# Attention with beacons and a gated feed-forward: start of the weight loads, the gate of the second batch's loads, and the cuts of the third batch

## Chip, cores and metric

The kernel runs on one core of one Trainium2 chip. The metric is the device time of one execution in microseconds; the times shown are medians of several runs. Besides, one execution was profiled, and every duration of a single instruction is from that one.

## The reference

Eight batches of eight heads, 576 positions, head size 64, and 16 beacon keys and values ahead of each sequence. The scores are causal over the 576 positions and open over the beacons. The result of all heads is put side by side and goes through a gated feed-forward with 1536 hidden columns.

```python
k_all = np.concatenate([beacon_k, k], axis=2)
v_all = np.concatenate([beacon_v, v], axis=2)
scores = scale * np.matmul(q, k_all.transpose(0, 1, 3, 2))
scores = np.where(causal, -1e9, scores)
a = np.exp(scores - scores.max(-1, keepdims=True))
a /= a.sum(-1, keepdims=True) + 1e-09
x = np.matmul(a, v_all)          # then [B*S, H*D] = [4608, 512]
out = (np.maximum(x @ w_gate, 0.0) * (x @ w_val)) @ w_out
```

## The kernel before

**Order of the work.** The whole kernel is a list of tasks, each with the engines that may run it, a cost in us, the tasks it depends on, the buffers it holds and a priority. When the program is built, a planner (class `Plan`, lines 134 to 244) plays the tasks through with these costs: it always takes the task that can start first, at equal times the one with the lowest priority number, and puts it at the end of its engine's queue. On the chip each engine works through its queue strictly in that order. So the costs in the code decide the order, and the chip decides the times: a task whose input comes later than planned holds up all that stands behind it on its engine. Where PE has a planned gap before 100 us, the planner puts in filler matmuls (line 874), which compute nothing.

**Loads.** All loads of q, k and v, the transposing DMAs and the stores are issued by SP, in one queue. For each batch there are four pairs of heads for k and four for q (`load_pair`, 256 KB in packets of 1 KB, so 256 packets), one rest each for k and q (`load_rest`, 80 rows of 8 heads in 256 B packets, so 640, in two DMAs each) and five for v (`load_v`, up to 128 rows of 8 heads, 1024 packets; the first one in two DMAs, beacon and v). Their order is "KQ0011v2233vvvv" for batch 1 and on: K and Q are the rests, a digit is a pair (first k, then q), v the next of the five. They land in seven shared fp32 stage buffers. From there POOL (for batch 0 POOL or DVE) rounds them to bf16: line 455 for k and q, line 415 (`copy`) for v. PE transposes k and q (line 467), ACT or DVE evict them (lines 411 and 413) into `kT` and the block-diagonal `diag`.

**Weights.** The nine weight blocks (three each of gate, value and output, in the order g0, v0, g1, v1, g2, v2, o0, o1, o2) are fetched and cast to bf16 by DMAs that POOL issues (line 428). The planner may issue block i no earlier than W_FROM + W_STEP * i. The rests of batch 1 wait for a weight: in the plan both rests have the weight `GATE` as dependency, and in the program the first DMA of the k rest has a semaphore wait on it (lines 524 to 526). `GATE` is ("v", 1), the fourth weight.

**Attention.** For each batch and each head pair the positions are cut into steps A to E of 128 rows (two heads of 64), and a step F for the last positions of all heads. A step is: scores on PE (line 628 or 620), minimum with mask on DVE (line 643), exponential on ACT (line 654), reciprocal (666) on DVE and normalisation on POOL, for batch 0 on POOL or DVE (673). The probabilities are then transposed, for batch 0 by PE (708), for the others by one transposing DMA per group of steps (719), and multiplied by v (729), and the result is copied to `xT` (411 or 413). `STEPS` says which steps form a group: for batches 0 and 1 "AB", then "C", then "D", "E", each for all four pairs. A batch that is not in `STEPS` does all five steps of a pair in one group, no earlier than 39 us per batch in the plan.

**Feed-forward.** For each batch the first 512 positions are cut by `CUTS` into parts of columns; a part can begin once the attention of those columns is in `xT` for all pairs. For each of 12 hidden blocks PE runs four matmuls with the gate weight and four with the value weight (line 796), ACT the relu (800), DVE the product (804). The projection (816) works on 128 rows at a time. The last 64 positions of four batches together form one more part. Its priority stands behind all attention, so it fills PE.

Of the kernel before, what the change touches and what calls it, by code (L numbers as in the profile page):

```python
# [20 lines left out]
RANK1 = -8.1  # L21
AHEAD = 2.0
W_ISSUE = 0.8
W_MOVE = 3.2
W_FROM = 14.0
W_STEP = 3.3
SHARED = 1.5
FILLED = 100.0
FILL = 0.8
FILL_FROM = 2.9  # L30
# [8 lines left out]
NORM_B = 1  # L39
N_DVE = 0.3  # L40
F_MOST = 3
GATE = "v", 1
SC_MOST = 4
SC_FIRST = 6
V_MOST = 3
# [3 lines left out]
N_ST = 7  # L49
N_OSB = 4  # L50
STEPS = {0: [(["AB"], 0.0, 0.6), (["C"], 2.4, 0.6), (["D", "E"], 4.8, 0.6)],
         1: [(["AB"], 0.0, 0.6), (["C"], 2.4, 0.6), (["D", "E"], 4.8, 0.6)]}
CUTS = {0: (240,), 1: (368,)}
LAST_PARTS = 2
FIRST_MOST = 3
PACE0 = 0.0
# [77 lines left out]
class Plan:  # L134
# [7 lines left out]
    def add(self, engines, cost, run, deps=(), holds=(), prio=0.0, lag=None, part=False, lazy=0.0, after=0.0, move=0.0):  # L142
        t = Task(engines if isinstance(engines, tuple) else (engines,), cost, run, deps, holds, prio, lag, part, lazy, move)
        t.ready = after
        for d in t.deps:
            d.users.append(t)
        self.tasks.append(t)
        return t

    def order(self):  # L150
# [10 lines left out]
        wire = cast = 0.0  # L161
# [16 lines left out]
        while True:  # L178
            best = None
            for e in queue:  # L180
                for t in queue[e]:
# [3 lines left out]
                    at, could = times  # L185
# [20 lines left out]
            t.start, t.engine = at, e  # L206
            cost = t.cost
            if e == "DMA":
                issue, move = cost
                rest = max(0.0, cast - max(wire, at + 0.3))  # L210
                cast += min(move, rest / SHARED)
                move += min(rest, SHARED * move)
                if issue > 1.2:
                    wire = max(wire, at + 0.3) + move
                    free[e] = max(at + issue, wire - 0.2)
                else:
                    free[e] = at + issue
                    wire = max(wire, at + issue) + move
                end = max(wire, free[e]) + 1.9
            elif t.move:  # L220
                free[e] = at + cost
                cast = max(cast, free[e] + 0.7) + t.move
                end = cast + 2.0
            else:
                if isinstance(cost, dict):
                    cost = cost[e]
                if e == "PE":
                    cost += SWITCH * (t.part != part)
                    part = t.part
                free[e] = end = at + cost  # L230
            for h in t.holds:
                h.users -= 1
                if h.users == 0:
                    h.slots.give(end + (0.1 if e == "DMA" else LAGS[e] if t.lag is None else t.lag), h.tile)
            done.append(t)
            for u in t.users:
                u.ready = max(u.ready, end + (LAGS[e] if t.lag is None else t.lag))
# [10 lines left out]
def kernel(  # L248
# [184 lines left out]
    def heads(src, b, s0, sl):  # L433
        return src[b, :, s0:s0 + sl, :].rearrange("h s d -> s h d")
# [6 lines left out]
    def new_batch(b, prio, work):  # L441
# [18 lines left out]
        def turned(h16, rows, ca, prio, users):  # L460
# [8 lines left out]

            return ps, add("PE", c_pe(4 * rows), turn, (ca, on_ident), (h16, ps), prio[1])  # L470

        eng = ("POOL", "DVE") if b == 0 else ("POOL",)
        cost = {"POOL": 0.6, "DVE": 0.55}
        MAIN = 4 * P
# [2 lines left out]
        def load_pair(kind, p, prio):  # L477
# [2 lines left out]
            st = Hold(stage_s, 2)  # L480

            def fetch(_):
                nc.sync.dma_start(st.tile.rearrange("p (h e) -> p h e", h=2),
                                  src[b, 2 * p:2 * p + 2, s0:s0 + MAIN, :].rearrange("h (p j) d -> p h (j d)", j=4))

            ld = add("DMA", (0.5, 0.87), fetch, (), (st,), prio[0])
            dst = t.kT if kind == "k" else t.diag
            h16, ca = rounded(dst, st, P, neg_scale if kind == "q" else 1.0, prio, ld,
                              lambda t_: t_.rearrange("p (j h d) -> p h j d", h=2, j=4))
# [23 lines left out]
        def load_rest(kind, prio):  # L513
# [5 lines left out]
            def fetch(_):  # L519
                s3 = st.tile.rearrange("p (h d) -> p h d", h=H)  # L520
                at = 0
                for src, s0, n in pieces:
                    one = nc.sync.dma_start(s3[at:at + n], heads(src, b, s0, n))  # L523
# [26 lines left out]
        def load_v(c, prio):  # L550
            st = Hold(stage_s, 2)
            rows = min(P, SK - P * c)

            def fetch(_):
                s3 = st.tile.rearrange("p (h d) -> p h d", h=H)
                if c == 0:
                    nc.sync.dma_start(s3[:Nb], heads(beacon_v, b, 0, Nb))
                    nc.sync.dma_start(s3[Nb:], heads(v, b, 0, P - Nb))
                else:
                    nc.sync.dma_start(s3[:rows], heads(v, b, P * c - Nb, rows))  # L560
# [347 lines left out]
```

## Time and profile before

| what | us |
|---|---|
| runs: median of 3 (lowest, highest) | 424.46 (424.33, 424.82) |
| the profiled execution | 423.93 |
| its span, first to last instruction | 422.2 |

In a row of the table by stage stand the stretch and its length in us, then for each engine its busy time with the number of instructions, then the granted clock of PE as a share of full speed, the mean share of the DMA engines and GB/s. In a row of the time line stand the start and the length in us, engine, line, operation, output and inputs, the shape and the number of instructions merged; in brackets, how long the engine had been idle and who released it. A row of the DMA view gives the KB of one transfer and the time from its issue to its landing.

### The profile page before, as it was taken

To read this page: it belongs to the slowest core of one execution; us is meant where nothing else is said; L and a number is where in the kernel's file an instruction comes from. 1 tells how busy PE (TensorE), PEld (TensorE's weight loads), DVE (VectorE), ACT (ScalarE), POOL (GpSimd) and SP (SyncE) were. 2 spreads that over 40 slices of the span, in tenths; PEclk is the share of its full clock that TensorE was granted. 3 is DMA by queue.
4 is the path that set the end of the run, shared out by engine and by line. 5 is a ranking of instruction groups with operands and counts; after the bars stand their busy time and mean duration, and the time that the engine had idled before them with its cause. 6 is when DMAs were issued, how large, how long until landed. Compare 5 with 4: busy or idle time off the path is not lost.

```text
span 422.2 us, 10131 instructions
## 1 busy us (share of the span) xinstructions
PE 399.7 (95%) x3194; PEld 234.9 (56%) x3229; DVE 318.5 (75%) x1147; ACT 290.0 (69%) x957; POOL 226.5 (54%) x421
## 2 busy tenths in 40 slices
PE   7878799999999999989999999999999999999994
PEld 4655677646657445544555765455454544444483
DVE  6788798888999987888988989889897334243251
ACT  5677799877988889778978998886788133023030
POOL 6676467766876868486866786686755000000000
PEclk9999999999999999999999999999999999999999
DMA  7999926999999999989997899898954600110112
GB/s 210 217 241 234 201 59 118 215 205 219 135 274 215 180 175 240 206 159 231 243 193 190 206 242 184 162 244 217 221 94 79 152 27 2 50 50 2 50 51 50
DMA packets 172486, 68.00 MB, mean 161 GB/s; under 512 B 146704, under 2 KB 167952, under 8 KB 172432
## 3 DMA queue, kind: packets, MB, share of 16 engines
q1 hardware_dynamic: 167680, 62.64, 70.0%
q0 software_dynamic: 4752, 4.72, 6.7%
q8 instruction: 25, 0.41, 0.4%
q14 instruction: 29, 0.24, 0.2%
HBM read 38.54 MB, written 9.44 MB: 114 GB/s over the span
## 4 chain that ended last, share of the span: by engine, by line
PE 51%; POOL 2%; DVE 1%; DMA 1%; issue 1%; SPq 1%; ACT 0%; POOLq 0%; DVEq 0%
PE f L796 27%; PE f L816 15%; PE f L729 3%; PE f L628 3%; PE f L467 2%; POOL pb L673 1%; DMA st<-in_q_dram 1%; PE f L620 1%; PE f L758 1%; SPq L523 0%; DVE osb L413 0%; DVE f L643 0%; POOL h L455 0%; SPq L560 0%; PE f L623 0%
## 5 line engine op out<-in xcount | busy, mean ns | idle before, releaser
L673 POOL TENSOR_SCALAR pb<-pb,small 128x448 bf16<-128x448 bf16 (+8 forms) x237 | 125.8, 545 | 58.1 <-DVE small L666 42.1
L654 ACT ACTIVATE pb<-f,small 128x512 bf16<-128x512 f32 (+3 forms) x272 | 137.5, 519 | 19.8 <-DVE small L643 11.6
L643 DVE CUSTOM_DVE_ANT_0 f<-f,mask 128x64 f32<-128x64 f32 (+7 forms) x256 | 112.4, 476 | 7.8 <-PE f L628 6.4
L800 ACT ACTIVATE g<-f 128x512 f32<-128x512 f32 (+5 forms) x144 | 69.5, 496 | 68.5 <-PE f L796 64.3
L796 PE MATMUL f<-xT,wg_r 128*128 128x512 bf16 (+5 forms) x567 | 109.3, 325 | 1.9 <-DVE xT L413 0.7
L796 PE MATMUL f<-xT,wv_r 128*128 128x512 bf16 (+5 forms) x565 | 110.4, 325 | 0.7 <-ACT pb L654 0.2
L804 DVE TENSOR_TENSOR hT<-g,f 128x512 bf16<-128x512 f32 (+5 forms) x144 | 79.0, 552 | 40.8 <-PE f L796 35.9
L816 PE MATMUL f<-wo_r,hT 128*128 128x512 bf16 (+1 forms) x429 | 100.7, 373 | 0.9 <-issue 0.3
L796 PEld LDWEIGHTS <-wg_r 128*128 128x128 bf16 x576 | 53.6, 98 | 37.8 <-issue 1.4
L796 PEld LDWEIGHTS <-wv_r 128*128 128x128 bf16 x576 | 52.8, 98 | 37.2 <-issue 0.8
L816 PEld LDWEIGHTS <-hT 128*128 128x128 bf16 x444 | 42.0, 98 | 41.7
L455 POOL TENSOR_SCALAR h<-st 128x512 bf16<-128x512 f32 (+1 forms) x80 | 48.9, 616 | 21.8 <-DMA st<-in_q_dram 6.3
L654 ACT ACTIVATION_READ_ACCUMULATOR pb<-f,small 128x1 f32 x272 | 57.9, 213 | 0.0
L628 PE MATMUL f<-kT,diag 128*128 128x64 bf16 (+7 forms) x256 | 47.1, 286 | 0.5 <-DVE kT L413 0.3
L413 DVE COPY osb<-f 128x512 f32<-128x512 f32 (+1 forms) x31 | 21.0, 681 | 27.8 <-PE f L816 22.7
L643 DVE DVE_READ_ACCUMULATOR2_ANT small<- 128x1 f32 x296 | 41.1, 139 | 0.3 <-issue 0.2
L467 PE MATMUL f<-ident,h 128*128 128x128 bf16 (+1 forms) x320 | 29.6, 220 | 6.9 <-POOL h L455 5.8
L467 PEld LDWEIGHTS <-h 128*128 128x128 bf16 (+1 forms) x320 | 21.3, 99 | 20.7 <-POOL h L455 12.8
L729 PEld LDWEIGHTS <-v 128*64 128x64 bf16 (+1 forms) x560 | 21.8, 109 | 14.8 <-issue 8.7
L413 DVE CAST diag<-f 64x512 bf16<-64x512 f32 (+2 forms) x48 | 25.8, 550 | 4.5 <-ACT diag L411 3.2
L640 DVE TENSOR_REDUCE small<-f 128x1 f32<-128x512 f32 x40 | 27.3, 682 | 1.0 <-PE f L620 0.5
L628 PEld LDWEIGHTS <-diag 128*128 128x128 bf16 x256 | 20.2, 98 | 13.9 <-DVE diag L413 0.6
(64 smaller groups left out, 357.3 us busy)
## 6 DMA issues: line engine op xcount, KB each, us to landing
st<-in_k_dram SPq DMA_DIRECT2D x32, 256.0 KB, 4.2
st<-in_q_dram SPq DMA_DIRECT2D x32, 256.0 KB, 4.1
out_dram<-osb SPq DMA_DIRECT2D x32, 256.0 KB, 2.4
st<-in_v_dram SPq DMA_DIRECT2D x24, 256.0 KB, 4.8
st<-in_v_dram SPq DMA_DIRECT2D x8, 224.0 KB, 5.3
wg_r<-in_moe_w_gate_dram POOLq DMA_DIRECT2D x3, 512.0 KB, 9.7
wv_r<-in_moe_w_val_dram POOLq DMA_DIRECT2D x3, 512.0 KB, 9.5
wo_r<-in_moe_w_out_dram POOLq DMA_DIRECT2D x3, 512.0 KB, 9.6
```

The lines of the kernel that those rows point to most:

```text
L413: nc.vector.tensor_copy(dst, src)
L455: e.tensor_scalar(order(h16.tile)[:rows], st.tile[:rows] if rows < P else st.tile.rearrange("p (h j d) -> p h j d", h=2, j=4), by, 1.0, AL ...
L467: nc.tensor.matmul(to, h16.tile[:rows, a * P:(a + 1) * P], ident[:rows, :rows], start=True, stop=True)
L628: nc.tensor.matmul(view(i), t.diag.tile[:, p, j * P:j * P + P], kT[:, p, :n], start=True, stop=True)
L643: nc.vector.tensor_tensor_reduce(out=view(i), in0=view(i), in1=msk, scale=1.0, scalar=small["t"][:, 0:1] if name in "EF" else 3.0e38, op0= ...
L654: nc.scalar.activation(ph.tile.rearrange("p a n -> p (a n)")[:, a:a + n], view(i), AF.Exp, bias=small["t"][:, low:low + 1], scale=-1.0, ac ...
L673: (nc.gpsimd if x.engine == "POOL" else nc.vector).tensor_scalar(one, one, small["t"][:, 8 + i:9 + i], 1.0, ALU.mult, ALU.mult)
L729: nc.tensor.matmul(ps.tile[64 * hh:64 * hh + 64, d0:d0 + w], t.v.tile[:rows, c, D * h:D * h + D], rhs(64 * hh), start=(c == 0), stop=(c == ...
L796: nc.tensor.matmul(to, w_r[:, ki, nf * P:(nf + 1) * P], x, start=(ki == 0), stop=(ki == KM - 1))
L800: r = add("ACT", c_act(w), lambda _, psg=psg, g=g: nc.scalar.activation(g.tile[:, :w], psg.tile[:, :w], AF.Relu), (a,), (psg, g), -1000 + ...
L804: hid.append(add("DVE", c_dve(w), lambda _, psv=psv, g=g, nf=nf: nc.vector.tensor_mul(hT[nf].tile[:, c0:c0 + w], g.tile[:, :w], psv.tile[: ...
L816: nc.tensor.matmul(ps.tile[:, :w], hT[nf].tile[:, t0:t0 + P], wo_r[:, nf, n0:n0 + w], start=(nf == 0), stop=(nf == NF - 1))
```

## The change

Weights: W_FROM goes from 14.0 to 17.0 and the planned move of one weight from 3.2 to 3.1 us. Gate: `GATE` becomes ("v", 0), the second weight, and now all 15 loads of batch 1 depend on it in the plan, not the two rests alone; in the program the DMAs of the pairs, the rests and the first or only DMA of each v load have the semaphore wait. Loads beside weights: the planner lengthened a load by up to 1.5 times its own move while a weight was still to move; now it lengthens it by 0.006 us for each of its packets, in proportion to how much of the load falls beside weights. Batches: the first part of batch 1's feed-forward ends at column 240 instead of 368, batch 2's feed-forward is cut at 240 too, and batch 2's attention is done in two groups per pair, "AB" for all pairs and then "C", "D", "E", with no earliest start. The stored end time `t.end` is not used.

```diff
-W_MOVE = 3.2
-W_FROM = 14.0
+W_MOVE = 3.1
+W_FROM = 17.0
 W_STEP = 3.3
-SHARED = 1.5
+PACKET = 0.006
...
-GATE = "v", 1
+GATE = "v", 0
...
 STEPS = {0: [(["AB"], 0.0, 0.6), (["C"], 2.4, 0.6), (["D", "E"], 4.8, 0.6)],
-         1: [(["AB"], 0.0, 0.6), (["C"], 2.4, 0.6), (["D", "E"], 4.8, 0.6)]}
-CUTS = {0: (240,), 1: (368,)}
+         1: [(["AB"], 0.0, 0.6), (["C"], 2.4, 0.6), (["D", "E"], 4.8, 0.6)],
+         2: [(["AB"], 0.0, 0.6), (["C", "D", "E"], 2.4, 0.6)]}
+CUTS = {0: (240,), 1: (240,), 2: (240,)}
...
             if e == "DMA":
-                issue, move = cost
-                rest = max(0.0, cast - max(wire, at + 0.3))
-                cast += min(move, rest / SHARED)
-                move += min(rest, SHARED * move)
+                issue, move, *packets = cost
+                slow = PACKET * (packets[0] if packets else 128)
+                both = min(1.0, max(0.0, cast - max(wire, at + 0.3)) / (move + slow))
+                cast += move * both
+                move += slow * both
...
+        gate = (weight_in[GATE],) if b else ()
+
+        def gated(one):
+            if b == 1:
+                tc.add_manual_dep(one.ins, weight_dma[GATE].ins.name, mybir.DependencyInfo(
+                    mybir.DependencyClass.Sync, mybir.DependencyReason.DATA), reason="weights first")
...
-            ld = add("DMA", (0.5, 0.87), fetch, (), (st,), prio[0])
+            ld = add("DMA", (0.5, 0.87, 256), fetch, gate, (st,), prio[0])
...
-                    one = nc.sync.dma_start(s3[at:at + n], heads(src, b, s0, n))
-                    if b == 1 and kind == "k" and at == 0:
-                        tc.add_manual_dep(one.ins, weight_dma[GATE].ins.name, mybir.DependencyInfo(
-                            mybir.DependencyClass.Sync, mybir.DependencyReason.DATA), reason="weights first")
+                    gated(nc.sync.dma_start(s3[at:at + n], heads(src, b, s0, n)))
                     at += n
 
-            ld = add("DMA", (1.3, 0.96), fetch, (weight_in[GATE],) if b == 1 else (), (st,), prio[0])
+            ld = add("DMA", (1.3, 0.96, 640), fetch, gate, (st,), prio[0])
...
-            ld = add("DMA", (1.1 if c == 0 else 0.55, 1.54 * rows / P), fetch, (), (st,), prio[0])
+            ld = add("DMA", (1.1 if c == 0 else 0.55, 1.54 * rows / P, 8 * rows), fetch, gate, (st,), prio[0])
```

In the plan the loads of the later batches depend on that weight as well (`if b`); in the program only batch 1's have the wait.

More of the change, by code (lines that the diff above doesn't have):

```diff
@@ L234, in order @@
                     h.slots.give(end + (0.1 if e == "DMA" else LAGS[e] if t.lag is None else t.lag), h.tile)
+            t.end = end
             done.append(t)
@@ L482, in fetch @@
             def fetch(_):
-                nc.sync.dma_start(st.tile.rearrange("p (h e) -> p h e", h=2),
-                                  src[b, 2 * p:2 * p + 2, s0:s0 + MAIN, :].rearrange("h (p j) d -> p h (j d)", j=4))
-            ld = add("DMA", (0.5, 0.87), fetch, (), (st,), prio[0])
+                gated(nc.sync.dma_start(st.tile.rearrange("p (h e) -> p h e", h=2),
+                                        src[b, 2 * p:2 * p + 2, s0:s0 + MAIN, :].rearrange("h (p j) d -> p h (j d)", j=4)))
+            ld = add("DMA", (0.5, 0.87, 256), fetch, gate, (st,), prio[0])
             dst = t.kT if kind == "k" else t.diag
@@ L556, in fetch @@
                 if c == 0:
-                    nc.sync.dma_start(s3[:Nb], heads(beacon_v, b, 0, Nb))
+                    gated(nc.sync.dma_start(s3[:Nb], heads(beacon_v, b, 0, Nb)))
                     nc.sync.dma_start(s3[Nb:], heads(v, b, 0, P - Nb))
                 else:
-                    nc.sync.dma_start(s3[:rows], heads(v, b, P * c - Nb, rows))
-            ld = add("DMA", (1.1 if c == 0 else 0.55, 1.54 * rows / P), fetch, (), (st,), prio[0])
+                    gated(nc.sync.dma_start(s3[:rows], heads(v, b, P * c - Nb, rows)))
+            ld = add("DMA", (1.1 if c == 0 else 0.55, 1.54 * rows / P, 8 * rows), fetch, gate, (st,), prio[0])
             t.rows["v", c] = add(eng, cost, lambda x: copy(x.engine, t.v.tile[:rows, c, :], st.tile[:rows]),
```

## The prediction

> **What bounds the kernel now.** I read the page first, then the busy time of the engines by stage, then who waited for whom on PE, POOL and DVE in the first 65 us, and last each load's issue and landing there.
>
> ```profile
> span 422.2 us, 10131 instructions
> PE 399.7 (95%) x3194; PEld 234.9 (56%) x3229; DVE 318.5 (75%) x1147; ACT 290.0 (69%) x957; POOL 226.5 (54%) x421
> ```
>
> PE is busy for 95% of the span, so a gain must come from PE time in which it does nothing or does filler work. The table by stage says where that is. I cut the span at 33.6 us (first feed-forward matmul), 64.8 us (first feed-forward matmul on the second part of batch 0) and 340 us (attention is over). The first four rows are all instructions; the last is the filler matmuls of line 874 alone, which compute nothing.
>
> ```profile
> 0.00:33.60 33.60, 26.83 (x263) 18.27 (x264) 26.07 (x122) 23.27 (x68) 21.23 (x45) 1.00 1.03 224
> 33.60:64.80 31.20, 26.37 (x305) 20.05 (x305) 25.33 (x97) 26.04 (x92) 20.12 (x34) 1.00 0.85 153
> 64.80:340.00 275.20, 269.92 (x2211) 155.96 (x2236) 238.13 (x883) 222.05 (x764) 185.15 (x343) 1.00 0.93 192
> 340.00:422.20 82.20, 76.55 (x421) 40.62 (x426) 28.94 (x48) 18.59 (x36) 0.00 (x0) 1.00 0.11 36
> ...
> 0.00:33.60 33.60, 17.08 (x100) 9.80 (x100) 1.00 1.03 224
> ```
>
> After 64.8 us PE idles 275.20 - 269.92 = 5.3 us up to 340 us and 5.7 us behind it, most of that the last output. There PE is the bound: work that arrives earlier only lengthens its backlog. Before 64.8 us PE idles 6.8 + 4.8 = 11.6 us, and up to 33.6 us it runs 100 fillers: there the attention of batch 0 feeds PE, and a stall of that chain moves the end. The clock (the 1.00 behind POOL) is full throughout, so no term is a clock term.
>
> Three idle stretches of PE are large, and each has a late load behind it. The next rows are of the time line, by engine: PE, then DVE, then POOL, then SP's issues.
>
> ```profile
> 23.71 0.36 PE L729 MATMUL f<-xT,v 128*64 128x128 bf16 x6 [1.45 <-DVE xT L413]
> 33.60 0.98 PE L796 MATMUL f<-xT,wg_r 128*128 128x240 bf16 x8
> 37.23 0.34 PE L708 MATMUL f<-ident,xT 128*128 128x128 bf16 x3 [1.72 <-POOL xT L673]
> 51.34 0.32 PE L467 MATMUL f<-ident,h 80*128 80x80 bf16 x4 [2.14 <-POOL h L455]
> 56.68 0.44 PE L628 MATMUL f<-kT,diag 128*128 128x64 bf16 x4
> 64.80 1.09 PE L796 MATMUL f<-xT,wg_r 128*128 128x272 bf16 x8
> ...
> 22.16 0.42 DVE L413 CAST v<-st 80x512 bf16<-80x512 f32 x1 [1.70 <-DMA st<-in_v_dram]
> ...
> 34.47 0.73 POOL L415 TENSOR_SCALAR v<-st 128x512 bf16<-128x512 f32 x1 [3.19 <-DMA st<-in_v_dram]
> 50.66 0.61 POOL L455 TENSOR_SCALAR h<-st 80x512 bf16<-80x512 f32 x1 [3.66 <-DVE small L643]
> ...
> 13.87 1.36 SPq L560 DMA_DIRECT2D st<-in_v_dram  x1
> 15.32 0.61 SPq L483 DMA_DIRECT2D st<-in_k_dram  x1
> 19.73 0.42 SPq L558 DMA_DIRECT2D st<-in_v_dram  x1
> 36.11 0.61 SPq L523 DMA_DIRECT2D st<-in_k_dram  x1
> ```
>
> The landings of those three loads, from the DMA view cut to the moment of their issue, with a load before any weight for comparison (last row):
>
> ```profile
> st<-in_v_dram SPq DMA_DIRECT2D x1, 160.0 KB, 8.3
> ...
> st<-in_v_dram SPq DMA_DIRECT2D x1, 224.0 KB, 14.6
> ...
> st<-in_k_dram SPq DMA_DIRECT2D x1, 128.0 KB, 13.6
> ...
> st<-in_v_dram SPq DMA_DIRECT2D x1, 256.0 KB, 6.9
> ```
>
> Stall A: batch 0's last v load, issued at 13.87, lands 8.3 us later at 22.2, where DVE had waited 1.70 us with the scores queued behind that copy; PE idles 1.45. Stall B: batch 1's first v load, issued at 19.73, lands 14.6 us later at 34.3; POOL stood 3.19 us before its copy at 34.47, batch 0's normalisations queued behind it, and PE idles 1.72. Stall C: batch 1's k rest, issued at 36.11, lands at 49.7, its beacon piece just after; POOL stood 3.66 us before the rounding at 50.66. The view names a DVE instruction as releaser there, but the landing fits and I put it down to the load. PE idles 2.14. In sum **5.31 us of PE idle** comes from loads that ran beside weights.
>
> **The change, part by part.** *Weights and gate.* These rows are the second weight's issue, which is the new gate, and the fourth's, the old gate; then SP's wait for the old gate and the second weight's landing.
>
> ```profile
> 17.62 0.79 POOL L428 DMA_DIRECT2D wv_r<-in_moe_w_val_dram  x1
> 25.77 0.79 POOL L428 DMA_DIRECT2D wv_r<-in_moe_w_val_dram  x1
> ...
> SPq L523 <- DMA wv_r<-in_moe_w_val_dram: 5.4, 1, 5.4
> ...
> wv_r<-in_moe_w_val_dram POOLq DMA_DIRECT2D x1, 512.0 KB, 9.5
> ```
>
> With W_FROM at 17.0 and a step of 3.3 the first weight goes out at about 17.0 and the second at 20.3. Batch 0's last v load then has neither a weight nor batch 1's loads beside it and should land in at most the 6.9 us of its larger neighbour: 20.8 instead of 22.2, 1.4 us earlier, which is nearly all of stall A. I take -1.45 (bounds -1.7, DVE's wait, and 0).
>
> The second weight lands at 20.3 + 9.5 = 29.8 at the latest and, with the engines nearly to itself, I expect 27 to 28. Until then SP issues nothing: behind its waiting instruction stand all 15 loads of batch 1, and behind those batch 2's and the transposes, the first at 63.3. So batch 1's first load goes out some 12 us later than 15.32, but its k and q rest, first in the list, some 8 us earlier than 36.11. Stall B goes: the first v load now stands behind rests and four pair loads. Stall C goes, since the rest is due by 28 + 13.6 = 41.6, 9 us before 50.66. -1.72 and -2.14.
>
> What is late next? POOL rounds batch 1's pairs in order among batch 0's normalisations, and those loads now run later and still beside seven weights. The planner's new rule (0.006 us for each packet beside a weight) expects 7.7 us for a v load of 1024 packets where the old one expected at most 3.9, 4.8 against 2.4 for a rest, 2.4 against 2.2 for a pair. The copies that came too early in POOL's order are just those of the loads whose expectation grows, so the order errs less, but not by nothing. Bounds: 0, and 5.31 again; I take one stall like B, **+1.72**, the row that is also a copy put ahead of its load.
>
> Three rows for what follows: batch 1's first values on PE, two of its evictions on ACT, and the busy times from 40 to 50 us.
>
> ```profile
> 68.89 0.36 PE L729 MATMUL f<-xT,v 128*64 128x128 bf16 x6
> 28.60 1.19 ACT L411 CAST diag<-f 64x512 bf16<-64x512 f32 x2
> 40.00:50.00 10.00, 9.03 (x98) 7.09 (x96) 9.84 (x37) 9.92 (x33) 4.34 (x7) 1.00 1.22 199
> ```
>
> Cover for lateness itself: batch 1's first scores ran at 56.68 and its first values at 68.89; when 64.8 comes PE has 96 x 0.116 + 36 x 0.216 = 18.9 us of batch 0's second part (strides below) in front of it. A shift by 12 us is covered by that; it costs where it blocks POOL's queue, not as missing work.
>
> Batch 1's evictions on ACT and DVE, those of 28.60 among them, move behind 33 us. ACT gets them back where it is as full (9.92 of 10 us), so I count 0; bounds -2.4 us (the two of that row and two more like them, ahead of batch 0's last exponentials) and +2.4.
>
> *Cuts.* The first row below is a run of eight matmuls, as are the rows at 33.60 and 64.80 above; the groups by shape give the mean ns of one, with its fill and drain. The stride is the run less one matmul's own time, over 7.
>
> ```profile
> 155.82 1.89 PE L796 MATMUL f<-xT,wg_r 128*128 128x512 bf16 x8
> ...
> L796 PE MATMUL f<-xT,wg_r 128*128 128x512 bf16 x279 | 70.0, 379 | 1.2 <-DVE xT L413 0.7
> L796 PE MATMUL f<-xT,wg_r 128*128 128x272 bf16 x48 | 6.9, 279 | 0.0
> L796 PE MATMUL f<-xT,wg_r 128*128 128x240 bf16 x48 | 6.4, 265 | 0.2 <-ACT pb L654 0.2
> ...
> L804 DVE TENSOR_TENSOR hT<-g,f 128x512 bf16<-128x512 f32 x72 | 49.3, 686 | 32.4 <-PE f L796 28.9 <-ACT pb L654 1.4 <-ACT g L800 0.8
> L804 DVE TENSOR_TENSOR hT<-g,f 128x272 bf16<-128x272 f32 x12 | 5.2, 436 | 1.0 <-PE f L796 0.8
> L804 DVE TENSOR_TENSOR hT<-g,f 128x240 bf16<-128x240 f32 x12 | 4.7, 401 | 2.1 <-PE f L796 1.5 <-PE f L874 0.4 <-ACT xT L411 0.2
> ```
>
> 512 columns: (1.89 - 0.379) / 7 = 216 ns. 240: (0.98 - 0.265) / 7 = 102; 272: (1.09 - 0.279) / 7 = 116. Batch 2 replaces 96 strides of 216 by 96 of 102 + 116 = 218: +0.2 us on PE. Batch 1 had 368 + 144 columns and gets 240 + 272; the stride goes with the columns (0.42 to 0.43 ns each in all three), so I count nothing. DVE gains 12 x (401 + 436 - 686) = 1.8 us, and ACT, with as many more relus, by my estimate about as much; from 64.8 to 340 us they idle 37 and 53 us. If that cover were gone, it would show as up to some 2 us.
>
> *Third batch in two steps.* Per head pair one transposing DMA of 25 blocks becomes one of 6 and one of 21.
>
> ```profile
> L719 SPq DMA_TRANSPOSE pTb<-pb x28: 1603/4018/6822, 81.2 to 327.7; - x28
> L719 SPq DMA_TRANSPOSE xT<-xT x8: 1209/1220/1919, 63.3 to 85.2; - x8
> ```
>
> SP gains four issues of 1.22 us (the six-block median), less what 21 blocks save on 25: between 2 and 5 us on a queue that mostly waits for POOL. The same score, softmax and value instructions run; batch 2's attention also loses its planned earliest start (78 us and later) and can fill holes before batch 1's is done. PE is bound there, so I count 0; bounds -1 (batch 2's first half no longer waits for the whole attention, part of the 5.3 us idle) and +2 (its work put in front of batch 1's on a full DVE).
>
> **Sum.** -1.45 - 1.72 - 2.14 + 1.72 + 0.2 = -3.4 us. The profiled execution took 423.93 us (span 422.2, 1.7 around it), 0.5 us under the median of 424.46; I apply the sum to both: 420.5 for a run like the profiled one, **421.0 us** for the median.
>
> **Rivals.** *Slower: the gate starves POOL.* If POOL's order has the first rounding of batch 1 well ahead of its landing, all normalisations of batch 0 stand behind one wait. Stalls B and C cost PE 1.72 / 3.19 = 0.54 and 2.14 / 3.66 = 0.58 us for each us that POOL stood. A POOL wait as long as the delay of the first load (about 12.7 us) would cost 0.58 x 12.7 = 7.4 us, and a second one like B 1.7: 9.1 + 0.2 - 5.3 = +4.0, 428.5 us. It decides from about 5.3 / 0.56 = 9.5 us of new POOL waits on. For it: between the end of batch 0's loads and the gate the engines carry little but two weights, and the same packets then have to move beside the other seven. Against it: stall A goes anyway, and the planner knows of the gate. The Trainium skill, DMA: Bandwidth & Descriptors, section Rules for kernel authors, tells authors to issue a DMA early and to wait late, which speaks against holding 15 loads back; stalls B and C were loads issued early that came late all the same, so this trace does not bear the rule out here, and the rival keeps a chance of its own.
>
> *No difference: the stalls only move.* New waits of about 5 us stand in the place of B and C, for instance for v loads that still land 14 us after issue: -5.3 + 5.1 + 0.2 = 0, 424.5 us. For it: seven of nine weights still overlap batch 1.
>
> *Faster still: batch 0 profits too.* No new stall, and the 2.4 us of ACT evictions leave the way of batch 0's first part: -5.3 - 2.4 + 0.2 = -7.5, 417.0 us. Against it: ACT and DVE are both full from 40 to 50 us and get that work back before 64.8.
>
> **Chances.** Forecast (418.5 to 423.5 by itself) 0.58; slower rival 0.22; no difference 0.10; faster still 0.10. A measurement of this kernel tells about 0.2%, 0.85 us, from no change: faster 0.68, same 0.10, slower 0.22. The range for 8 in 10 runs from 417.0, the sum without new stalls, to 427.0, most of the way to the slower rival.
>
> **What would show it.** Right: on SP no issue between 15.3 and about 27; POOL's first weight near 17; no DVE wait for v near 20; the rounding of 80 rows (L455) for batch 1 before 42; the first 272-column matmul of L796 at about 61 instead of 64.8; PE idle before that down from 11.6 to about 8 us. The idle from there to 340 us should stay near 5.3. Wrong: a POOL wait over 5 us for a load of batch 1 between 28 and 60 us, or a first 272-column matmul no earlier than 64.8. I would also be wrong if the stalls go, but PE idles over 2 us more between 100 and 200 us, where batch 2 changed.

## The result and the profile after

The changed kernel takes **420.64 us** (median of 5, 419.32 to 421.9) against 424.46 (median of 5, 423.68 to 427.24) of the kernel before, run beside it: ratio 0.9895 [0.9854, 0.9936]. Run again, beside the kernel before, it took 421.13 against 425.33, ratio 0.9911 [0.9881, 0.9942] (12 runs). The profiled execution took 420.64 us, span 418.9.

The head of its page, then its table by stage over the cuts that the prediction used (busy time and count of PE, PEld, DVE, ACT, POOL, then the granted clock, DMA share and GB/s):

```profile
span 418.9 us, 10398 instructions
...
PE 402.9 (96%) x3319; PEld 248.4 (59%) x3319; DVE 321.5 (77%) x1174; ACT 289.6 (69%) x953; POOL 226.4 (54%) x422
```

```profile
0.00:33.60 33.60, 29.36 (x266) 20.80 (x266) 27.86 (x130) 24.60 (x75) 20.79 (x45) 1.00 0.93 182
33.60:64.80 31.20, 27.11 (x318) 21.00 (x319) 26.54 (x105) 24.18 (x81) 20.25 (x35) 1.00 1.02 211
64.80:340.00 275.20, 273.04 (x2318) 167.20 (x2317) 239.60 (x896) 223.15 (x766) 185.38 (x343) 1.00 0.93 192
```

PE is idle for 4.2 + 4.1 = 8.3 us up to 64.8 us (before: 11.6) and 2.2 us from there to 340 (before: 5.3). Part of that second difference is bookkeeping: the page of before lists 35 matmuls fewer than weight loads (3194 against 3229), the page of after none, and a missing record reads as idle time.

Now the time line of after, by engine as in the prediction: PE, POOL, DVE, then SP's issues. L803 is the feed-forward matmul, L470 the transposes, L458 the rounding, L418 and L416 the copies, L431 the weights.

```profile
28.70 0.57 PE L803 MATMUL f<-xT,wg_r 128*128 128x240 bf16 x4
34.89 0.32 PE L470 MATMUL f<-ident,h 80*128 80x80 bf16 x4 [1.75 <-POOL h L458]
38.80 0.32 PE L470 MATMUL f<-ident,h 80*128 80x80 bf16 x4 [1.43 <-POOL h L458]
60.88 0.63 PE L803 MATMUL f<-xT,wg_r 128*128 128x272 bf16 x4
...
18.41 0.93 POOL L431 DMA_DIRECT2D wg_r<-in_moe_w_gate_dram  x1
21.34 0.79 POOL L431 DMA_DIRECT2D wv_r<-in_moe_w_val_dram  x1
34.22 0.61 POOL L458 TENSOR_SCALAR h<-st 80x512 bf16<-80x512 f32 x1 [2.56 <-DMA st<-in_beacon_k_dram]
38.14 0.61 POOL L458 TENSOR_SCALAR h<-st 80x512 bf16<-80x512 f32 x1 [2.06 <-DMA st<-in_q_dram]
50.15 0.64 POOL L418 TENSOR_SCALAR v<-st 128x512 bf16<-128x512 f32 x1
...
21.31 0.41 DVE L416 CAST v<-st 80x512 bf16<-80x512 f32 x1
...
8.66 6.94 SPq L567 DMA_DIRECT2D st<-in_v_dram  x4
27.38 0.61 SPq L533 DMA_DIRECT2D st<-in_k_dram  x1
```

Stalls A and B are gone: the last v copy of batch 0 and the first v copy of batch 1 carry no bracket, so nothing was waited for, and SP issues nothing between batch 0's last v load and 27.38. Stall C is gone at its old time, but the rounding that it held, of batch 1's k rest, now stands at 34.22 instead of 50.66 and waits again: POOL stands 2.56 us for the k rest and 2.06 for the q rest, PE 1.75 and 1.43 behind it. The landings (the DMA view, cut to each issue) show both sides: batch 0's last v load took 8.3 us before, the second weight 9.5 and the rest 13.6.

```profile
st<-in_v_dram SPq DMA_DIRECT2D x1, 160.0 KB, 4.9
...
wv_r<-in_moe_w_val_dram POOLq DMA_DIRECT2D x1, 512.0 KB, 6.0
...
st<-in_k_dram SPq DMA_DIRECT2D x1, 128.0 KB, 5.3
```

The first 272-column matmul comes at 60.88 instead of 64.80, 3.9 us earlier; from there to the end it is 358.0 us against 357.4. So the gain was made before 61 us and kept after it. That it was *kept* turned out to be the part that needed explaining.

### The profile page after: what moved, and what is told of

Same layout as the page of the kernel before. It is cut to its first block, busy times and chain, and to the rows that moved or that the text cites. A ratio compares the mean times of both kernels' runs of the same rounds, so it can differ in the third digit from the quotient of the medians.

```text
span 418.9 us, 10398 instructions
## 1 busy us (share of the span) xinstructions
PE 402.9 (96%) x3319; PEld 248.4 (59%) x3319; DVE 321.5 (77%) x1174; ACT 289.6 (69%) x953; POOL 226.4 (54%) x422
## 4 chain that ended last, share of the span: by engine, by line
PE 77%; DVE 7%; ACT 5%; DMA 5%; POOL 3%; issue 2%; SPq 1%; POOLq 0%; DVEq 0%; ACTq 0%
PE f L803 38%; PE f L823 21%; PE f L635 6%; PE f L736 5%; PE f L470 3%; DMA st<-in_q_dram 2%; DVE diag L416 2%; DVE f L650 2%; PE f L627 1%; ACT xT L661 1%; POOL pb L680 1%; DMA xT<-xT 1%; PE f L881 1%; DVE hT L811 1%; ACT pb L661 1%
## 5 line engine op out<-in xcount | busy, mean ns | idle before, releaser
L680 POOL TENSOR_SCALAR pb<-pb,small 128x512 bf16<-128x512 bf16 (+8 forms) x220 | 119.3, 556 | 71.1 <-DVE small L673 52.6
L661 ACT ACTIVATE pb<-f,small 128x64 bf16<-128x64 f32 (+4 forms) x256 | 130.9, 524 | 19.8 <-DVE small L650 12.8
L807 ACT ACTIVATE g<-f 128x512 f32<-128x512 f32 (+3 forms) x156 | 71.6, 470 | 71.2 <-PE f L803 69.2
L650 DVE CUSTOM_DVE_ANT_0 f<-f,mask 128x256 f32<-128x256 f32 (+7 forms) x256 | 112.6, 475 | 8.0 <-PE f L635 6.2
L803 PE MATMUL f<-xT,wv_r 128*128 128x512 bf16 (+3 forms) x624 | 113.0, 314 | 0.2 <-ACT xT L661 0.2
L803 PE MATMUL f<-xT,wg_r 128*128 128x512 bf16 (+3 forms) x624 | 110.5, 314 | 0.1
L811 DVE TENSOR_TENSOR hT<-g,f 128x512 bf16<-128x512 f32 (+3 forms) x156 | 80.2, 519 | 33.9 <-PE f L803 30.1
L803 PEld LDWEIGHTS <-wg_r 128*128 128x128 bf16 x624 | 59.7, 98 | 32.7 <-issue 0.2
L803 PEld LDWEIGHTS <-wv_r 128*128 128x128 bf16 x624 | 58.2, 98 | 34.4 <-issue 1.8
L458 POOL TENSOR_SCALAR h<-st 128x512 bf16<-128x512 f32 (+1 forms) x80 | 48.9, 617 | 15.0 <-DMA st<-in_q_dram 5.7
L635 PE MATMUL f<-kT,diag 128*128 128x256 bf16 (+7 forms) x256 | 48.4, 291 | 1.7 <-DVE diag L416 1.4
L650 DVE DVE_READ_ACCUMULATOR2_ANT small<- 128x1 f32 x296 | 41.2, 139 | 0.2
L416 DVE COPY osb<-f 128x512 f32<-128x512 f32 (+1 forms) x30 | 20.3, 679 | 24.0 <-PE f L823 23.4
L470 PE MATMUL f<-ident,h 128*128 128x128 bf16 (+1 forms) x320 | 30.1, 222 | 4.8 <-POOL h L458 4.4
L416 DVE CAST diag<-f 64x512 bf16<-64x512 f32 (+2 forms) x54 | 26.3, 505 | 7.9 <-PE f L470 4.4
L470 PEld LDWEIGHTS <-h 128*128 128x128 bf16 (+1 forms) x320 | 22.5, 101 | 16.1 <-POOL h L458 7.8
L661 ACT ACTIVATE xT<-f,small 128x64 bf16<-128x64 f32 (+3 forms) x64 | 27.4, 444 | 2.8 <-DVE small L650 2.2
```

What stands on the lines that cost most here:

```text
L416: nc.vector.tensor_copy(dst, src)
L458: e.tensor_scalar(order(h16.tile)[:rows], st.tile[:rows] if rows < P else st.tile.rearrange("p (h j d) -> p h j d", h=2, j=4), by, 1.0, AL ...
L470: nc.tensor.matmul(to, h16.tile[:rows, a * P:(a + 1) * P], ident[:rows, :rows], start=True, stop=True)
L635: nc.tensor.matmul(view(i), t.diag.tile[:, p, j * P:j * P + P], kT[:, p, :n], start=True, stop=True)
L650: nc.vector.tensor_tensor_reduce(out=view(i), in0=view(i), in1=msk, scale=1.0, scalar=small["t"][:, 0:1] if name in "EF" else 3.0e38, op0= ...
L661: nc.scalar.activation(ph.tile.rearrange("p a n -> p (a n)")[:, a:a + n], view(i), AF.Exp, bias=small["t"][:, low:low + 1], scale=-1.0, ac ...
```

## The experiments

Theory at the start: the later weights and the held loads make the whole gain in the first 65 us, and cuts and steps are worth nothing. Rival: the cuts and the two steps of batch 2 make it, or part of it. All the measured times first. "First" is the start of the first 240-column and first 272-column feed-forward matmul of the profiled execution, "rest" its span less the latter. These three columns come from one execution, which can lie up to 2.4 us from the median (e6's took 415.62 us, e14's 419.26, e1's 427.41).

| kernel | median us | ratio to before | first 240 | first 272 | rest |
|---|---|---|---|---|---|
| before | 424.46 | | 33.60 | 64.80 | 357.4 |
| after | 420.64 | 0.9895 [0.9854, 0.9936] | 28.70 | 60.88 | 358.0 |
| r_after | 421.13 | 0.9911 [0.9881, 0.9942] | 27.23 | 60.56 | 358.2 |
| e1_loads | 425.81 | 1.0007 [0.9972, 1.0041] | 28.79 | 62.01 | 363.7 |
| e2_cuts | 424.32 | 0.9977 [0.9949, 1.0006] | 35.16 | 65.28 | 357.2 |
| e3_hold | 428.0 | 1.0058 [1.0023, 1.0092] | 32.61 | 63.61 | 362.4 |
| e4_weights | 425.62 | 1.001 [0.9975, 1.0045] | 28.19 | 64.42 | 358.1 |
| e14_nocut | 421.44 | 0.9919 [0.9892, 0.9946] | 27.35 | 59.30 | 358.3 |
| e10_w14 | 421.26 | 0.9926 [0.9902, 0.995] | 31.90 | 59.99 | 361.0 |
| e11_oldgate | 426.58 | 1.0036 [1.0008, 1.0064] | 29.47 | 67.25 | 357.6 |
| e6_gate_v1 | 418.01 | 0.9861 [0.9826, 0.9896] | 27.34 | 53.12 | 360.8 |
| e7_oldrule | 420.36 | 0.9905 [0.9883, 0.9928] | 27.90 | 60.61 | 357.1 |
| e12_rest | 418.0 | 0.9856 [0.983, 0.9882] | 27.32 | 60.13 | 357.6 |
| e13_g0 | 414.56 | 0.9768 [0.9741, 0.9795] | 27.64 | 55.36 | 356.7 |

**e1_loads: weights, gate and packet rule of the change, old steps and cuts.** The changed kernel less

```diff
-         2: [(["AB"], 0.0, 0.6), (["C", "D", "E"], 2.4, 0.6)]}
-CUTS = {0: (240,), 1: (240,), 2: (240,)}
+CUTS = {0: (240,), 1: (368,)}
```

> The changed kernel, but with the cuts and steps of before (batch 1 cut at 368, batch 2 neither cut nor in two steps); weights, gate and the planner's rule as changed. Load theory (the gain is all made before 64.8 us, by the held loads): 420.5 to 421.2 us, the first feed-forward matmul at 28.7 us and the first 272-column one near 61, as in the changed kernel. Cut theory (a good part of the gain is the second and third batch's finer cuts): 422.5 us or more, with PE idle of 2 us or more from 120 to 200 us as before.

Measured: 425.81 us, no gain at all, although the first 272-column matmul came 2.8 us earlier than before (62.01). My theory fell with it. The table by stage from 120 to 160 us shows where the lead went: e1, then before, then after.

```profile
120.00:160.00 40.00, 36.05 (x335) 21.92 (x337) 34.09 (x145) 34.12 (x123) 29.16 (x55) 0.91 0.93 192
```

```profile
120.00:160.00 40.00, 38.28 (x353) 23.06 (x354) 37.37 (x147) 35.12 (x128) 29.32 (x56) 1.00 1.06 205
```

```profile
120.00:160.00 40.00, 39.47 (x361) 28.22 (x359) 35.80 (x140) 34.24 (x119) 28.21 (x52) 1.00 1.00 203
```

PE idles 4.0 us in e1, 1.7 in before and 0.5 in after; and e1's granted clock is 0.91, worth 40 x 0.09 = 3.6 us. e1 reached batch 1's feed-forward 2.3 us ahead of before (91.97 against 94.28) and batch 2's 2.6 us behind it (146.97 against 144.39). The same stretch of e1 in steps of 2 us, PE alone:

```profile
140.00:142.00 2.00, 1.64 (x32) 1.00 1.09 275
142.00:144.00 2.00, 0.81 (x3) 1.00 0.47 173
144.00:146.00 2.00, 1.35 (x17) 0.88 0.00 0
146.00:148.00 2.00, 1.26 (x4) 0.50 1.10 206
148.00:150.00 2.00, 2.00 (x6) 0.50 1.10 204
150.00:152.00 2.00, 2.00 (x9) 0.50 0.67 140
152.00:154.00 2.00, 2.00 (x10) 0.91 0.71 160
```

With batch 1's feed-forward done PE has nothing but the tail of batch 2's attention, runs dry, and the clock drops to half and stays there for some 6 us. The idle time is 2.9 us (8.00 less 5.06 in the first four rows), and the clock adds about as much again. This execution lies 1.6 us above e1's median. That the clock is lost in others too shows in its mean over all runs: about 0.990 in e1, 0.994 in the kernel before beside it and 0.995 in e14 below.

**e2_cuts: the kernel before with the new steps and cuts alone**, the same lines turned round.

> The kernel before with the cuts and steps of the change alone. Load theory: 424.2 to 424.8 us, stalls A, B and C (1.45, 1.72 and 2.14 us of PE idle) all still there. Cut theory: 422.5 us or less, PE idle from 120 to 200 us down from 3 us to under 1.

Measured: 424.32 us, 0.9977 [0.9949, 1.0006]: within what can be told. So neither half of the change makes the gain by itself, and both together do: the rival, taken as a sum of parts, falls as well.

**e3_hold: the kernel before with only the hold**, that is the gate on the second weight for all of batch 1's loads, weights as before (14.0 and 3.2), old rule, steps and cuts.

```diff
-GATE = "v", 1
+GATE = "v", 0
...
-            ld = add("DMA", (1.3, 0.96), fetch, (weight_in[GATE],) if b == 1 else (), (st,), prio[0])
+            ld = add("DMA", (1.3, 0.96, 640), fetch, gate, (st,), prio[0])
```

> The kernel before with one thing changed: all 15 loads of batch 1 wait for the second weight; weights still from 14 us, the planner's old rule, old cuts and steps. If holding the loads is what works, through the way it leaves free for batch 0's first part: first feed-forward matmul at 30 us or earlier and 421 to 422.5 us. If the later weights or the new rule are needed: first feed-forward matmul not before 32 us, POOL waits of over 5 us in sum for loads of batch 1 between 25 and 60 us, 424 us or more.

Measured: 428.0 us, slower by 0.58% [0.23, 0.92]. Its first 272-column matmul is 1.2 us early and its rest 5 us longer, as in e1: a lead without the two steps is lost, and more. Its first 240-column matmul, at 32.61, is only 1.0 us early. Its table from 120 to 160 us has the same two marks, 3.5 us of idle time on PE and a lowered clock:

```profile
120.00:160.00 40.00, 36.48 (x349) 22.34 (x352) 36.24 (x140) 32.88 (x121) 29.30 (x55) 0.96 1.02 198
```

**e4_weights: the kernel before with the weights' start alone.**

```diff
-W_MOVE = 3.2
-W_FROM = 14.0
+W_MOVE = 3.1
+W_FROM = 17.0
```

> The kernel before with one thing changed: weights from 17 us with a planned move of 3.1. If stall A came from the weight beside batch 0's last v load, it goes: the DVE wait near 20 us falls from 1.70 to under 0.5 us, first feed-forward matmul near 32 us, 423 us. If it came as much from batch 1's loads, which still go out from 15.3 us on: DVE still waits 1 us or more there, the first feed-forward matmul stays at 33 us or later, 424.5 us or more, since the old gate comes later too.

Measured: 425.62 us, 1.001 [0.9975, 1.0045]. Stall A goes by this alone; the rows are of the time line (DVE, POOL, PE):

```profile
19.95 0.42 DVE L413 CAST v<-st 80x512 bf16<-80x512 f32 x1
...
31.62 0.61 POOL L415 TENSOR_SCALAR v<-st 128x512 bf16<-128x512 f32 x1 [3.84 <-DMA st<-in_v_dram]
...
34.42 0.61 PE L467 MATMUL f<-ident,h 128*128 128x128 bf16 x4 [3.70 <-POOL h L455]
36.63 0.60 PE L467 MATMUL f<-ident,h 128*128 128x128 bf16 x4 [1.60 <-POOL h L455]
```

The first feed-forward matmul comes at 28.19, 5.4 us earlier. Then POOL stands for batch 1's first v, PE idles 3.70 and 1.60 us, and PE's clock falls to between 0.50 and 0.67 from 32 to 40 us. At the first 272-column matmul 0.4 us is left. Stall B has grown, from 1.72 us of idle time on PE, and with the clock behind it eats the gain from stall A. Stall C does not show here: both rests are rounded at 53.99 with no wait.

**r_after and e14_nocut: the changed kernel again, and with the two steps but the old cuts** (`CUTS = {0: (240,), 1: (368,)}`).

> The changed kernel again, beside the kernel before and the next three on this chip, as yardstick. Both theories: 420.5 to 422 us, ratio about 0.99, mean clock 0.995 or more, since no idle stretch of PE before the end is longer than about 2 us.

> The changed kernel with the cuts of before (batch 1 at 368, batch 2 uncut) but batch 2's attention still in two steps. Supply theory (PE, once it is ahead, runs out of feed-forward work near 140 us, because batch 2's attention ends on DVE and ACT near 145 us whatever the loads do, and only the cut at 240 lets batch 2's feed-forward begin before that): first feed-forward matmul of batch 2 at 143 us or later, PE idle of 2 us or more between 136 and 150 us, 423.5 to 426.5 us. Rival, the two steps or the mere other order are what helped: it starts near 136 us or PE idles under 1 us there, 421 to 422 us.

Measured: 421.13 and 421.44 us, 0.9911 and 0.9919. The cuts are worth nothing that can be told, so it is not the cut that lets batch 2's feed-forward begin in time. e14 is e1 plus one line, batch 2's two steps, and it is 0.9919 [0.9892, 0.9946] where e1 is 1.0007 [0.9972, 1.0041]: the two steps are worth 0.9% when the ramp is early. How they do it shows in the masked scores on DVE, the front of all attention (L649 in e1, L650 in e14; one row is up to 100 us, one from there to 140): e1, then e14.

```profile
0.00:100.00 100.00, 34.12 (x157) 0.98 0.95 193
100.00:140.00 40.00, 18.68 (x81) 1.00 1.00 203
```

```profile
0.00:100.00 100.00, 37.55 (x176) 1.00 0.97 196
100.00:140.00 40.00, 18.20 (x76) 1.00 0.94 198
```

By 100 us e14 has done 3.4 us more of them, and then both go on at one pace. Batch 2's first feed-forward matmul starts at 138.22 in e14 and at 146.97 in e1, and e14's PE is busy through:

```profile
120.00:160.00 40.00, 38.73 (x310) 22.16 (x310) 36.80 (x140) 34.62 (x121) 28.40 (x53) 1.00 0.93 199
```

Taking out batch 2's planned earliest start by itself leaves e1's program as it is, so it is the split and not the start time that lets the order put scores forward. The rows do not tell the batches apart; that the scores put forward are batch 2's is read from the earlier start of its feed-forward.

**e10_w14: the changed kernel with the weights at their old place** (e4's edit turned round).

> The changed kernel with weights from 14 us and a planned move of 3.2, as before; gate, rule, cuts and steps as changed. If the later weights are what lets batch 0's first part start early (28.2 us with the weights alone, 32.6 us with the hold alone): first feed-forward matmul at 31.5 us or later and 422.5 to 425 us. If the hold is enough beside the new rule: 30 us or earlier and 421 to 422 us.

Measured: 421.26 us, 0.9926 [0.9902, 0.995], as the changed kernel. Stall A is back (DVE waits 1.51 us for the same load, the first feed-forward matmul is at 31.90), yet the first 272-column matmul is at 59.99. The later weights are not needed beside the other parts. Its time line shows what takes their 3 to 5 us back: the second weight goes out at 18.00 instead of 21.34, the rests go out at 24.94 instead of 27.38, and both are rounded, at 32.16 and 34.82, with no wait. By these rows the later weights remove stall A and, through the later gate, bring the wait for the rests; e13 below, whose gate opens earlier too, has no such wait either. Behind 60 us e10 does not keep its lead whole: its rest is 361.0 us, and PE idles 2.5 us between 64.8 and 120 us, against 0.3 in the changed kernel. The two steps do not save every lead.

**e11_oldgate: the changed kernel without the hold**: only the rests wait, for the fourth weight, as before.

```diff
-GATE = "v", 0
+GATE = "v", 1
...
-        gate = (weight_in[GATE],) if b else ()
+        gate = (weight_in[GATE],) if b == 1 else ()
...
-            ld = add("DMA", (0.5, 0.87, 256), fetch, gate, (st,), prio[0])
+            ld = add("DMA", (0.5, 0.87, 256), fetch, (), (st,), prio[0])
```

> The changed kernel with the gate of before: only the two rests of batch 1 wait, and for the fourth weight; weights from 17 us, the new rule, cuts and steps as changed. If the hold is needed to keep POOL from standing: first feed-forward matmul still near 28.5 us, then POOL waits of 4 us or more in sum for loads of batch 1 and PE idle of 4 us or more between 28 and 45 us, with the clock down for a time if one stretch is longer than about 3 us: 422.5 to 425 us. If the new rule alone puts POOL's order right: under 2 us of such PE idle, 420.5 to 421.5 us.

Measured: 426.58 us, 1.0036 [1.0008, 1.0064]; beside r_after on the same chip the hold is worth 426.58 - 421.13 = 5.45 us. The time line of e11 (POOL, PE) has one large wait:

```profile
29.18 0.63 POOL L418 TENSOR_SCALAR v<-st 128x512 bf16<-128x512 f32 x1
40.94 0.62 POOL L418 TENSOR_SCALAR v<-st 128x512 bf16<-128x512 f32 x1 [5.23 <-DMA st<-in_v_dram]
...
42.93 0.82 PE L715 MATMUL f<-ident,xT 128*128 128x128 bf16 x6 [5.14 <-POOL xT L680]
```

This is not stall B. Batch 1's first v load landed in 6.5 us and its copy, the first row, waits for nothing; the rests too, rounded from 51.12 on, are not waited for. The wait is for the *second* v load, issued at 27.18 and landed 13.7 us later. POOL stands 5.23 us in front of its copy, and the normalisations behind it hold PE for 5.14; the clock drop that follows is shown in the last section. In the changed kernel the same load goes out at 45.24, takes 11.8 us and is copied at 60.23 with no wait: it is hardly faster, but the planner has put its copy where it is due. The Trainium skill, DMA: Bandwidth & Descriptors, section Rules for kernel authors, would issue early and wait late. Here other work stands behind the waiting copy in POOL's queue, and the measurement decides for holding.

**e6_gate_v1, e7_oldrule, e12_rest, e13_g0: the changed kernel with one line changed.** In order: all 15 loads held to the fourth weight (`GATE = "v", 1`); the old SHARED rule in place of the packet rule; batch 1's rests entered with 1100 packets instead of 640, so that the plan expects them later; all loads held to the *first* weight only (`GATE = "g", 0`).

> The changed kernel with all 15 loads of batch 1 held until the fourth weight instead of the second, some 6 us later. If the prediction's slower rival (the gate starves POOL) decides by the length of POOL's waits: SP's first load of batch 1 at 34 us or later, and either POOL waits over 9 us in sum for these loads and 424 us or more, or, if the planner moves batch 1's roundings back with the gate, POOL waits of 3 to 6 us as before and 420.5 to 422.5 us, since batch 1's attention has some 15 us to spare before its feed-forward begins at 91 us.

> The changed kernel with the planner's old rule for loads beside weights (up to 1.5 times a load's own move, not by packets). If the rule by packets is needed to put POOL's order right: POOL waits for loads of batch 1 between 25 and 60 us of 8 us or more in sum (4.7 us in the changed kernel), first 272-column matmul at 62.5 us or later, 422.5 us or more. If the hold and the two steps do it all: 420.5 to 421.5 us.

> The changed kernel, the planner told that batch 1's two rests have 1100 packets instead of 640, so that it expects them later. In the changed kernel POOL stands 2.6 and 2.1 us before the roundings of these rests, and PE 1.75 and 1.43 us. If those waits are on the path: they fall by half or more, first 272-column matmul near 59.5 us, 419 to 420 us. If the time only moves to the next wait, or PE's lead is lost again near 140 us: 420.5 to 421.5 us.

> The changed kernel with the gate on the first weight instead of the second, so that batch 1's loads go out near 24 us. If the rests land earlier while POOL's order has them at the same place: POOL waits for loads down to 2 us or less, 419 to 420 us. If the earlier loads slow the second weight and batch 0's first part: first feed-forward matmul at 29.5 us or later, 421 to 423 us.

Measured: e6 418.01, e7 420.36, e12 418.0, e13 **414.56** us. The packet rule is not needed (e7). Holding even longer does not starve POOL (e6: SP's first load of batch 1 at 31.99, POOL's waits for its loads 0.85, 0.73 and 1.96 us), which answers the slower rival in its own place. e12 gains about 0.5% over the changed kernel. Of the two waits it aimed at, POOL's for the k rest is 0.29 us and for the q rest 3.90; but in r_after, the same program as after, they are 1.09 and 3.24 against 2.56 and 2.06, so one trace does not tell what the edit did to them. I can't say by which reordering e12 gains, and for e6 the share of hold and order is open as well. This limits what any one pair of kernels shows: each edit makes the planner lay out the whole order anew, and an order can be worth 0.5% for no reason that was found. A difference of that size counts here only where a trace shows the wait behind it.

e6 and e12 came out faster than anything that was expected of them. So did e13, and it is faster than both kernels: 0.9768 [0.9741, 0.9795]. Its time line, SP's first held issue and POOL's rounding of the rests, and its table by stage:

```profile
23.03 0.61 SPq L533 DMA_DIRECT2D st<-in_k_dram  x1
...
30.59 0.62 POOL L458 TENSOR_SCALAR h<-st 80x512 bf16<-80x512 f32 x1
32.60 0.63 POOL L458 TENSOR_SCALAR h<-st 80x512 bf16<-80x512 f32 x1
```

```profile
0.00:33.60 33.60, 29.96 (x287) 21.67 (x288) 28.65 (x133) 25.66 (x79) 23.26 (x49) 1.00 0.98 202
33.60:64.80 31.20, 29.70 (x348) 23.02 (x346) 30.13 (x120) 27.68 (x94) 21.77 (x40) 1.00 1.05 201
```

The rests go out 27.38 - 23.03 = 4.35 us earlier than in after and are rounded with no bracket: the new stall of the change is gone too. PE idles 3.6 + 1.5 = 5.1 us up to 64.8 instead of 8.3, and the first 272-column matmul comes at 55.36. The idle time is about half of the gain: the span is 418.9 - 412.1 = 6.8 us shorter, of which 3.2 us is PE's idle time up to 64.8, 1.2 its idle time from there to 340, and 2.4 less busy time of PE, which was not explained.

## Why the prediction came out right, point by point

**The number.** 421.0 was forecast, 420.64 and 421.13 were measured. The first 272-column matmul was forecast for about 61 and PE's idle time before it at 8; they are 60.88 and 8.3. The mechanism of the ramp was right in kind: stalls behind late loads shrink, and the work behind them moves forward, which shows in the traces. But two of its sizes were off, one stall did not go the way that was told, and one step beyond the ramp was wrong. That the number still came within 0.4 us is in part luck, as the points below show.

**Stall A, -1.45: mis-sized, and then without effect.** The load landed in 4.9 us and DVE's wait went, as said. But the first feed-forward matmul moved by 4.9 us (5.4 with the weights alone, e4). The step took PE's idle time as the price. PE's idle is no measure of a stall there, since fillers occupy PE, and ACT shows more. Between 22 and 28 us ACT is busy 3.74 of 6 us in before and 6.00 in after:

```profile
22.00:28.00 6.00, 4.25 (x53) 2.94 (x52) 5.84 (x26) 3.74 (x17) 4.15 (x8) 1.00 1.19 228
```

```profile
22.00:28.00 6.00, 5.81 (x69) 4.14 (x66) 5.82 (x27) 6.00 (x20) 5.03 (x11) 1.00 1.21 190
```

By the first 272-column matmul nothing of it is left that the other parts would not have given: e10, with stall A, gets there at 59.99, since it does not have the wait for the rests.

**Stalls B and C, -1.72 and -2.14: gone, but not by the hold alone.** With the hold B goes (in e3 too: the first v copy, at 46.64, waits for nothing). But C goes with the later weights alone (e4), and in e11 neither B nor C is there, although nothing but the rests is held. What the hold keeps away there is a wait of B's kind at the next v load, 5.23 us on POOL; e11 puts the hold's whole worth at 5.45 us. For C the prediction took the rounding to stay at about 50.66, 9 us behind the landing. The planner moved it up with the loads, to 34.22 in the trace, so a wait came back at the same rounding.

**The new stall, +1.72: right in kind, mis-sized.** It was expected as one stall like B for a copy put ahead of its load. It came as two at the rests, 1.75 + 1.43 = 3.2 us, inside the bounds of 0 and 5.31; in r_after it is one of 2.62 us with a clock drop worth 1.7 behind it. With it the four stalls sum to -1.45 - 1.72 - 2.14 + 3.18 = -2.1 us; PE's idle time fell by 11.6 - 8.3 = 3.3, so some 1.2 us more came from small waits that the prediction did not list. The two misses nearly cancel, and that is luck. POOL's new waits of 4.6 us stayed well under the 9.5 at which the slower rival decides.

**Cuts, +0.2: right** within the measurement (e14 against r_after).

**"After 64.8 us PE is the bound ... work that arrives earlier only lengthens its backlog", with the two steps at 0: this step failed.** It holds for a backlog that lasts, and it does not last: it ends near 140 us, when batch 1's feed-forward is done and batch 2's attention is not. In e1, the loads' part alone, the lead ends there in idle time and half clock, and 425.81 is the result where this step would have given about 421. The two steps are worth 4.4 us beside the loads (425.81 against 421.44, on two chips; as ratios to the kernel before, 1.0007 and 0.9919 with intervals apart) and too little to tell alone. The bounds of -1 and +2 did not hold that. The prediction's last sign of being wrong, over 2 us more idle time on PE between 100 and 200 us, appears in e1 (4.0 us against 1.7 from 120 to 160), without the change to batch 2 that it was ascribed to. The number came out since both halves were in the change: the steps keep the gain that I counted as kept in any case. For the prediction that was luck.

**The rivals.** No difference was the fate of each half alone (e1, e2, e4), for another reason than the rival's in e1. Slower appeared in e3, for the most part at 140 us and not through POOL, and in e11, through POOL but for want of the hold. "Faster still" was right that the ramp held more: e13 took it, about half of it by losing the rests' stall.

## What to carry to other kernels

A lead won early is worth only what the bound engine's supply can carry: look for the next place where its backlog ends, and move that forward in the same change; test the parts both alone and together, since here each alone gave nothing. In this kernel, loads that were held and planned as held did better than loads issued early and awaited at the wrong place in an engine's queue (e11 against the changed kernel). Where fillers keep the bound engine busy, its idle time does not tell how far a stall moves the first useful matmul (1.45 us of idle time here, 4.9 us of movement); look at the engine that feeds it too, and ask whether a later wait takes the gain back.

## What the runs showed of the hardware

In these runs a lull on PE can cost more than its length. Between 20 and 65 us, the longest single idle time in before (2.14, stall C) and in after (1.75) left the clock at 1.00. r_after, the same program as after, had one wait of 2.62 us at the rounding of the q rest, with little work ahead of it; PE alone:

```profile
34.00:36.00 2.00, 0.46 (x8) 1.00 1.14 281
36.00:38.00 2.00, 0.93 (x12) 1.00 1.15 303
38.00:40.00 2.00, 2.00 (x19) 0.62 1.21 220
40.00:42.00 2.00, 2.00 (x17) 0.53 1.20 254
42.00:44.00 2.00, 2.00 (x26) 1.00 1.18 260
```

The clock fell to 0.62 and 0.53 for 4 us, 4 x 0.42 = 1.7 us of lost pace, after the gap and not in it. In e11 it was as much, around the end of the 5.14 us that PE waited:

```profile
40.00:42.00 2.00, 0.00 (x0) 1.00 1.17 245
42.00:44.00 2.00, 1.07 (x9) 0.57 0.96 140
44.00:46.00 2.00, 2.00 (x13) 0.57 1.18 184
46.00:48.00 2.00, 2.00 (x28) 1.00 1.23 222
```

The Trainium skill, TensorE: Matmul & The Clock Gate, section Part 1: The HAM clock gate (the "warmup" mystery), has the clock halve after at least one idle window of about 3.4 us that runs freely, and come back after a busy one; e11 agrees. But in r_after PE was busy for 1.39 of the 4 us ahead of the drop and in e1 for 5.06 of the 8 around it, so here the window need not be wholly idle. Nor does the length of one gap decide: e3 fell to 0.63 and 0.52 between 40 and 44 us with no single wait over 1.37 us, PE having been busy for 2.10 of the 4 us up to 40.5, while before kept 1.00 with 1.86 of 4 us busy up to 51.5. That a busier stretch loses the clock and a less busy one does not fits a window that runs freely; it does not prove one. Added up in the same way, the drops between 20 and 65 us and between 120 and 160 come in two sizes: 1.7 us of lost pace in r_after, e7, e11, e12, in e1 near 40 us and in e3 near 40 and near 147, and twice that, 3.4, in e4 and in e1 near 148. Before, after, e2, e6, e10, e13 and e14 have none there.

Loads and weights slow each other. Batch 0's last v load, 160 KB, landed in 4.9 us with neither weights nor batch 1's loads beside it (after), in 6.2 beside batch 1's loads, with weights moving only at its very end (e4), in 7.4 and 7.9 beside weights alone (e3, e10) and in 8.3 beside both (before). The second weight took 6.0 us with no load beside it (after) and 9.5 beside loads (before). Some loads took much longer, 14.6 us for batch 1's first v load in before; there the loads ahead of it in the same queue count too, and no run parts the two.
